# Up products of one block by Strassen's scheme, with VectorE work moved to make room for them

## The chip, the cores and the metric

The kernel runs on one core of a Trainium2 chip. A core has TensorE (PE, with its weight loads shown apart as PEld), VectorE (DVE), ScalarE (ACT), GpSimd (POOL), SyncE (SP) and 16 DMA engines. The metric is the device time of one execution in microseconds, lower is better.

## The reference, cut to what matters

A layer norm feeds two branches, and their sum with the input is the output. One branch is a diagonal complex state-space model over 2048 tokens, the other a gated feed-forward layer:

```python
def _B_ref(x, w1, w3, w2):
    gate = jnp.einsum("bsd,df->bsf", x, w1)      # 2048 x 512 times 512 x 1792
    up = jnp.einsum("bsd,df->bsf", x, w3)
    h = _silu(gate) * up
    return jnp.einsum("bsf,fd->bsd", h, w2)
# ... _A_ref: Bu = xn B_bar; h_t = Lam_bar h_{t-1} + Bu_t; y = 2 Re(C h) + Dskip xn
xn = _layernorm(x, axis=-1)
return x + _A_ref(xn, ...) + _B_ref(xn, ...)
```

## The kernel before

The tokens are cut into four blocks (0 to 3) of 512. For a block, 14 gate tiles and 14 up tiles of 128 features are computed, each by four matmuls of 512 columns. The inputs of the recurrence (the `bu` stage) are eight more tiles of four such matmuls in each block. The outputs are computed for pairs of 128-token chunks; there are eight pairs (0 to 7), two for each block. This last stage already uses Strassen's scheme, with seven products in place of eight.

```python
def mms(ps, w, f, tsl):                       # in glu(b): one gate or up tile
    for dt in range(NDT):                     # NDT = 4
        nc.tensor.matmul(out=ps[:, tsl], lhsT=w[:, dt, f * P:(f + 1) * P], rhs=xnT[:, dt, tsl], ...)
...
g_ps = ...; mms(g_ps, w1_sb, f, slice(0, TBLK))
u_ps = ...; mms(u_ps, w3_sb, f, slice(0, TBLK))
evac(f, g_ps, u_ps)                           # ACT: Silu of the one, Copy of the other
```

The sums for the output stage are made by VectorE, S1 among them, and S1 is used by the second product of a pair:

```python
def row_sums(n, b, p):
    ...
    return [... for out, x, z, op in ((s1, a21, a22, ALU.add), (a21, a11, a21, ALU.subtract),
                                      (s2, s1, a11, ALU.subtract))]
```

The recurrence is rotated into real scans by products with tables. A rotation uses a work buffer `p` of two (`ssmw`), and its sum is mostly made by a DMA that accumulates into its destination, so as to spare VectorE:

```python
st["p"] = ssmw.tile(FULL, BF16, name="p")                              # pre_a: waits until p is free
nc.vector.tensor_tensor(out=st["p"][...], in0=st["g"], in1=tabe[...], op=ALU.mult)
...
gp.dma_start(out=st["g"], in_=st["p"], accum_op=ALU.add)               # pre_c, blocks 1 to 3
...
gp.dma_start(out=act_state(b, hf), in_=st["p16"], accum_op=ALU.add)    # post_c, all blocks
```

The order of VectorE's work is set by the program: a small list scheduler in it (`bg`) decides where the background work of the recurrence, the residual and the sums stands.

## Time and profile before

| | before |
|---|---|
| median of 3 runs | 203.59 us (203.54 to 204.22) |
| span of the profiled execution | 202.6 us (that execution took 204.41 us, 0.8 over the median) |
| PE busy | 97% |
| DVE busy, first to last stretch | nearly full until about 162 us, then half idle |

First the busy shares of the whole execution from the page, and the slice rows of PE and DVE (40 slices of about 5 us; 9 is 90% or more).

```profile
PE 197.4 (97%) x1304; PEld 122.5 (60%) x1317; DVE 172.5 (85%) x242; ACT 125.1 (62%) x251; POOL 44.2 (22%) x68
...
PE   8899999999999999999999999999999999999994
...
DVE  3699699999999999989949999999999935584833
```

PE has no slack, and from slice 6 to slice 32 DVE has little (slice 21 holds the wait shown below). To see the stages, here are busy times in windows of the same execution. The columns are: window, its length, then busy time and number of instructions of PE, PEld, DVE, ACT and POOL (instructions that reach over an edge are counted, too), granted clock, DMA share, GB/s. The five windows are pairs 0 and 1; gate/up and recurrence inputs of block 2, with recurrence inputs of block 3; pairs 2 and 3; gate/up of block 3; pairs 4 and 5.

```profile
69.99:86.80 16.81, 16.81 (x156) 15.04 (x154) 16.45 (x24) 12.00 (x31) 5.67 (x6) 1.00 0.55 110
86.80:124.78 37.98, 37.77 (x174) 17.24 (x177) 35.01 (x37) 28.98 (x52) 7.86 (x8) 1.00 0.51 91
124.78:141.59 16.81, 16.81 (x155) 15.06 (x154) 16.71 (x24) 2.38 (x6) 2.58 (x3) 1.00 0.55 111
141.59:165.77 24.18, 24.02 (x112) 10.96 (x112) 21.84 (x26) 16.39 (x28) 3.45 (x4) 1.00 0.46 93
165.77:182.58 16.81, 16.81 (x155) 15.06 (x154) 10.69 (x18) 2.66 (x7) 0.00 (x0) 1.00 0.09 25
```

DVE is busy for 16.71 of 16.81 us right before the stage that the change rewrites, for 21.84 of 24.18 us in it, and for only 10.69 of 16.81 us after it. Two pairs take 16.81 us of matmuls when PE never waits; this number serves as the ruler below.

The chain that ended last, in order of time (start, length, what), runs through PE alone in block 3:

```profile
141.81 10.74 PE gu_ps L525 x49
152.55 0.05 issue
152.60 10.95 PE gu_ps L525 x50
163.56 0.05 issue
163.61 2.32 PE gu_ps L525 x10
```

DVE's waits show one for a work buffer that an accumulating DMA still reads (columns: who waited for whom, total us, times, longest):

```profile
DVE p L457 <- DMA act<-p: 2.6, 1, 2.6
```

### The profile page before, as it was taken

The page shows a single profiled execution, that of the slowest core. Times are in us where ns is not written, and L with a number is a line of the kernel's source. Part 1 is how long each engine was busy: PE and PEld are TensorE (multiplying, and loading weights), DVE is VectorE, ACT ScalarE, POOL GpSimd, SP SyncE. Part 2 cuts the span into 40 slices and gives each one's busy share as a digit, 9 for nine tenths or more (in the row PEclk, how much of TensorE's full clock was granted, in tenths as well). Part 3 has the DMA queues.
Part 4 walks back from the last instruction along what each step waited for, and adds up shares of the span by engine and source line. Part 5 has one row for each costly group of instructions (what it writes and reads, how often), then busy time and mean ns, then how long its engine had stood idle before and what let it go on. Part 6 is the DMA issues. An engine that isn't in the chain of part 4 may idle for free.

```text
span 202.6 us, 3438 instructions
## 1 busy us (share of the span) xinstructions
PE 197.4 (97%) x1304; PEld 122.5 (60%) x1317; DVE 172.5 (85%) x242; ACT 125.1 (62%) x251; POOL 44.2 (22%) x68
## 2 busy tenths in 40 slices
PE   8899999999999999999999999999999999999994
PEld 2774444444444588854444446888444458888993
DVE  3699699999999999989949999999999935584833
ACT  4699797699999966788866676110576662101010
POOL 7070279700310043352111010310101110000000
PEclk9999999999999999999999999999999999999999
DMA  6999996990573043926796004566330780101011
GB/s 165 320 258 217 290 172 143 319 273 2 101 146 66 0 78 74 170 98 106 93 188 125 11 19 88 99 135 133 91 65 0 153 160 1 52 3 52 29 40 39
DMA packets 28816, 23.16 MB, mean 114 GB/s; under 512 B 16128, under 2 KB 26496, under 8 KB 28800
## 3 DMA queue, kind: packets, MB, share of 16 engines
q1 hardware_dynamic: 25536, 13.21, 26.7%
q0 software_dynamic: 2688, 9.44, 24.9%
q10 hardware_dynamic: 576, 0.30, 0.5%
q8 instruction: 10, 0.16, 0.3%
q14 instruction: 6, 0.05, 0.1%
HBM read 7.74 MB, written 2.10 MB: 49 GB/s over the span
## 4 chain that ended last, share of the span: by engine, by line
PE 94%; DMA 2%; SPq 1%; DVE 1%; issue 1%
PE gu_ps L525 45%; PE gu_ps L724 16%; PE y_ps L724 9%; PE bu_ps L724 7%; PE y_ps L435 7%; PE bu_ps L435 7%; DMA w_sb<-in_B_w_dram 2%; PE gu_ps L557 2%; PE bu_ps L557 1%; DVE xn L735 1%; SPq L161 0%; PE y_ps L238 0%; SPq L151 0%; DVE x_blk L735 0%; SPq L163 0%
## 5 line engine op out<-in xcount | busy, mean ns | idle before, releaser
L525 PE MATMUL gu_ps<-xnT,w_sb 128*128 128x512 bf16 x415 | 91.9, 379 | 0.5
L525 PEld LDWEIGHTS <-w_sb 128*128 128x128 bf16 x424 | 41.4, 98 | 49.4
L724 PEld LDWEIGHTS <-act 128*128 128x128 f16 x451 | 43.2, 98 | 5.5
L534 ACT ACTIVATE g<-gu_ps 128x512 bf16<-128x512 f32 x55 | 33.1, 601 | 13.2 <-PE gu_ps L525 12.6
L535 ACT ACTIVATE u<-gu_ps 128x512 bf16<-128x512 f32 x55 | 33.2, 603 | 9.8 <-PE gu_ps L525 9.5
L435 PEld LDWEIGHTS <-bt 128*128 128x128 bf16 x128 | 12.5, 98 | 15.1
L543 DVE TENSOR_TENSOR act<-g,u 128x1024 f16<-128x1024 bf16 x28 | 19.0, 678 | 3.1 <-ACT u L535 3.1
L478 DVE TENSOR_TENSOR_SCAN u<-rho,act,u 128x512 bf16<-128x512 f32 x16 | 19.6, 1269 | 0.0
L492 POOL DMA_DIRECT2D act<-p x8 | 7.1, 887 | 42.3 <-DVE act L488 30.9
L435 PE MATMUL y_ps<-xnT,bt 128*128 128x512 bf16 x63 | 15.1, 379 | 0.1
L435 PE MATMUL bu_ps<-xnT,bt 128*128 128x512 bf16 x61 | 14.8, 379 | 0.1
L457 DVE TENSOR_TENSOR p<-u,tabe 128x2048 bf16<-128x2048 bf16 x8 | 9.8, 1221 | 2.7 <-DMA act<-p 2.6
L468 POOL DMA_DIRECT2D u<-p x6 | 5.3, 876 | 27.5 <-ACT u L535 7.9
L724 PE MATMUL y_ps<-tw,act 128*128 128x256 f16 x88 | 10.9, 273 | 0.0
L724 PE MATMUL gu_ps<-w_sb,act 128*128 128x256 bf16 (+1 forms) x84 | 10.8, 268 | 0.0
L724 PE MATMUL gu_ps<-tw,act 128*128 128x256 f16 x88 | 10.7, 273 | 0.0
L437 ACT ACTIVATE u<-bu_ps 128x512 bf16<-128x512 f32 x16 | 9.4, 597 | 2.0 <-PE bu_ps L435 1.6
L437 ACT ACTIVATE u<-y_ps 128x512 bf16<-128x512 f32 x16 | 9.5, 597 | 1.8 <-PE y_ps L435 1.3
L744 ACT ACTIVATE bu_ps<-y_ps 128x256 f32<-128x256 f32 x4 | 1.5, 369 | 13.7 <-PE y_ps L724 13.7
L461 DVE TENSOR_TENSOR u<-u,tabe 128x2048 bf16<-128x2048 bf16 x8 | 9.8, 1222 | 0.2
L478 DVE TENSOR_TENSOR_SCAN u<-rho,ends,u 128x512 bf16<-128x512 f32 x8 | 9.9, 1269 | 0.0
L484 DVE TENSOR_TENSOR p<-u,tabe 128x2048 f16<-128x2048 bf16 x8 | 9.8, 1221 | 0.1
(146 smaller groups left out, 279.6 us busy)
## 6 DMA issues: line engine op xcount, KB each, us to landing
act<-p POOLq DMA_DIRECT2D x8, 512.0 KB, 4.8
u<-p POOLq DMA_DIRECT2D x6, 512.0 KB, 4.9
xn<-x_blk POOLq DMA_DIRECT2D x4, 512.0 KB, 5.6
out_dram<-xn SPq DMA_DIRECT2D x15, 128.0 KB, 1.7
w_sb<-in_B_w_dram SPq DMA_DIRECT2D x1, 1792.0 KB, 7.9
w_sb<-in_B_w_dram SPq DMA_DIRECT2D x2, 768.0 KB, 6.3
w_sb<-in_B_w_dram SPq DMA_DIRECT2D x4, 256.0 KB, 4.9
w_sb<-in_B_w_dram SPq DMA_DIRECT2D x2, 512.0 KB, 6.2
```

Of the source, the lines that this page charges most:

```text
L435: nc.tensor.matmul(out=ps, lhsT=bt[:, ri, dt, pt * P:(pt + 1) * P], rhs=xnT_blk[b][:, dt, :], start=(dt == 0), stop=(dt == NDT - 1))
L437: nc.scalar.activation(out=u[:, j, ri, :], in_=ps, func=ACT.Copy)
L457: nc.vector.tensor_tensor(out=st["p"][:, :, ::-1, :], in0=st["g"], in1=tabe[:, psl, 2:0:-1, :], op=ALU.mult)
L461: nc.vector.tensor_tensor(out=st["g"], in0=st["g"], in1=tabe[:, psl, 0:1, :].to_broadcast(FULL), op=ALU.mult)
L478: nc.vector.tensor_tensor_scan(out=v, data0=rho[:, pt:pt + 1].to_broadcast([P, TBLK]), data1=v, initial=init, op0=ALU.mult, op1=ALU.add)
L484: nc.vector.tensor_tensor(out=st["p16"][:, :, ::-1, :], in0=st["g"], in1=tabe[:, psl, 1:3, :], op=ALU.mult)
L492: gp.dma_start(out=act_state(b, hf), in_=st["p16"], accum_op=ALU.add)
L525: nc.tensor.matmul(out=ps[:, tsl], lhsT=w[:, dt, f * P:(f + 1) * P], rhs=xnT[:, dt, tsl], start=(dt == 0), stop=(dt == NDT - 1))
L534: nc.scalar.activation(out=g16[:, f % 2, :], in_=g_ps, func=ACT.Silu)
L535: nc.scalar.activation(out=u16[:, f % 2, :], in_=u_ps, func=ACT.Copy)
L543: nc.vector.tensor_tensor(out=act(b)[:, k0:k1 + 1:k1 - k0, :], in0=g16, in1=u16, op=ALU.mult)
L724: nc.tensor.matmul(out=out, lhsT=left[:, k, :], rhs=right[k][:, cols], start=(start and k == 0), stop=(k == NK - 1), skip_group_check=True)
```

## The change

The intent is to save PE time in block 3. Twelve of its 14 up tiles form three groups of four tiles: 512 features by 512 inputs by 512 tokens, each halved. Strassen's scheme computes the group with seven products of half size in place of eight. A product is 2 x 2 matmuls of 256 columns. The sums of weights (S) and of tokens (T) are new VectorE work, and so are the sums of products that are read from PSUM, the memory that matmuls write. Accumulation in PSUM and copies by ScalarE do the rest of the recombination.

```diff
+    def up_sums(b):                          # on DVE: T1..T4 (128x512), S1..S3 (128x1536, all three groups)
+        ...
+    def glu_last(b):
+        def product(out, left, right, start):
+            for h in range(2):
+                for k in range(2):
+                    nc.tensor.matmul(out=out[:, h * TH:(h + 1) * TH], lhsT=left[:, k, h * P:(h + 1) * P],
+                                     rhs=right[:, k, :], ...)          # TH = 256 columns
+        ...                                   # tiles 12 and 13 as before
+        for n in range(NG):                   # NG = 3 groups; between the products stand the four gate tiles
+            product(g, a11, b11, True);  copy(f, g)
+            product(e, s1n, t1, True);   copy(s5, e)
+            gate_side(f0, upper[0])
+            product(f, a12, b21, False)
+            product(g, s2n, t2, False);  copy(e, g)
+            nc.vector.tensor_tensor(out=s4n, in0=a12, in1=s2n, op=ALU.subtract)
+            copy(upper[1][:, :, 0:TH], halves(f))
+            gate_side(f0 + 1, upper[0])
+            product(g, s3n, t3, False);  copy(z, g);  add(lower[1][:, :, TH:TBLK], g)
+            product(e, s4n, b22, False); add(upper[1][:, :, TH:TBLK], e)
+            gate_side(f0 + 2, lower[0])
+            product(z, a22, t4, False);  copy(lower[1][:, :, 0:TH], halves(z))
+            gate_side(f0 + 3, lower[0])
```

The rest makes room on VectorE and in time. S1 of pairs 2 to 5 is added in place by an accumulating DMA; S3 and S2 are formed without it; the products of pairs 2 to 7 stand in another order, so that S1 is used in the fifth product in place of the second (S2 stays in the fourth, which is now the first to need one of these sums). Three rotation buffers lie in blocks of `x` that are free by then. Two rotation sums go back to VectorE, and background work is put at other places:

```diff
+        return [(0.9, subtract(s3, a11, a21), ("sums", n)),
+                (0.9, lambda: ...vector add a21 += a22...) if n in (0, 1, 6, 7) else
+                (0.0, lambda: gp.dma_start(out=a21, in_=a22, accum_op=ALU.add), ("sums", n)),
+                (0.9, subtract(s2, a22, s3), ("sums", n))]
...
+        for i in ((1, 5, 2, 6, 4, 3, 7) if b == 0 else (1, 4, 2, 6, 5, 7, 3)):
+            products[i - 1]()                 # before: 1, 5, 2, 6, 4, 3, 7
...
-                st["p"] = ssmw.tile(FULL, BF16, name="p")
+                if b == NBLK - 1 or (b, hf) == (2, 1):
+                    st["p"] = x_blk[2 if b == 2 else 2 + hf].rearrange("p (j r) t -> p j r t", r=2)
+                else:
+                    st["p"] = ssmw.tile(FULL, BF16, name="p")
...
-                if b == 0:                    # pre_c on VectorE
+                if b == 0 or (b, hf) == (2, 0):
...                                           # post_c of (3, 1) on VectorE, too
+            if b == 0:
+                held.append((cl, o))          # stores of block 0 are issued after pair 1
```

More of the change, by code (lines that the diff above doesn't have):

```diff
@@ L95 @@
     MID = 8
+    NG = 3
+    TH = TBLK // 2
     LEAD = 2.0
@@ L125 @@
     bt = const.tile([P, 2, NDT, PS], BF16, name="bt")
+    bt_flat = bt.rearrange("p r t d -> p (r t d)")
     ct = const.tile([P, NPT, 2, D], FP16, name="ct")
@@ L441, in bu, with ssm_tasks @@
             bg.fill()
-    def ssm_tasks(b, posts_last=False, between=()):
+    def ssm_tasks(b, posts_last=False, between=(), middle=(), late=()):
         FULL = [P, 2, 2, TBLK]
@@ L491, in post_c @@
             def post_c():
-                gp.dma_start(out=act_state(b, hf), in_=st["p16"], accum_op=ALU.add)
+                if (b, hf) == (NBLK - 1, 1):
+                    nc.vector.tensor_tensor(out=act_state(b, hf), in0=act_state(b, hf), in1=st["p16"], op=ALU.add)
+                else:
+                    gp.dma_start(out=act_state(b, hf), in_=st["p16"], accum_op=ALU.add)
             pre_a.ready = lambda: (b, hf) in u_blk
@@ L498, in ssm_tasks @@
         (pre0, scans0, post0), (pre1, scans1, post1) = (half(hf) for hf in range(NPT // 2))
-        transfers = (post0[2], post1[2]) + ((pre0[2], pre1[2]) if b > 0 else ())
+        transfers = (post0[2],) + (() if b == NBLK - 1 else (post1[2],)) + ((pre1[2],) if b > 0 else ()) + ((pre0[2],) if b in (1, 3) else ())
         def add(*fns):
@@ L508, in ssm_tasks @@
             return
-        add(*pre0, *pre1)
+        add(*pre0)
+        for t in middle:
+            bg.add(*t)
+        add(*pre1)
         for t in between:
@@ L512, in ssm_tasks @@
         add(*scans0)
+        for t in late:
+            bg.add(*t)
         if posts_last:
@@ L606, in glu @@
             evac(f, g_ps, u_ps)
-            if b in (1, NBLK - 1) and f == NFT - 3:
-                seeds(0 if b == 1 else 4)
+            if b == 1 and f == NFT - 3:
+                seeds(0)
+            if b == 2 and f == 1:
+                bg.first(res_list(2))
             if b == 0 and f == FIRST:
@@ L613, in glu @@
             bg.tensor(1.72)
-            bg.fill()
+            bg.fill((4.0 if f < NFT - 3 else 1.0) if b == 2 else None)
             if pend and f % 2 == 0:
@@ L617, in glu, with up_quarter @@
         return gate
-    def res_tasks(b):
+    def up_quarter(kh, r, half=False):
+        v = w3_sb[:, 2 * kh:2 * kh + 2, 0:4 * NG * P].rearrange("p k (g r f) -> p k g r f", g=NG, r=2)[:, :, :, r, :]
+        return v.bitcast(FP16) if half else v
+    ups = {}
+    def up_sums(b):
+        xnT = xnT_blk[b]
+        n = 4 * NG * P
+        at = 2 * TBLK
+        s1, s2 = (bt_flat[:, at + i * n:at + (i + 1) * n].bitcast(FP16).rearrange("p (k g f) -> p k g f", k=2, g=NG)
+                  for i in range(2))
+        a11, a21, a22 = up_quarter(0, 0), up_quarter(0, 1), up_quarter(1, 1)
+        s3 = up_quarter(0, 1, True)
+        t = xtp.tile([P, NDT, TBLK], BF16, name="xnT").bitcast(FP16).rearrange("p a (k t) -> p a k t", k=2)
+        t1, t2, t3, t4 = (t[:, i] for i in range(4))
+        b11, b12, b21, b22 = (xnT[:, 2 * i:2 * i + 2, j * TH:(j + 1) * TH] for i in range(2) for j in range(2))
+        ups.update(s=(s1, s2, s3, up_quarter(1, 0, True)), t=(t1, t2, t3, t4), b=(b11, b12, b21, b22),
+                   s5=bt_flat[:, 0:2 * TBLK].bitcast(FP32))
+        return [(cost, lambda out=out, x=x, z=z, op=op: nc.vector.tensor_tensor(out=out, in0=x, in1=z, op=op), "up")
+                for cost, out, x, z, op in ((0.45, t1, b12, b11, ALU.subtract), (0.95, s1, a21, a22, ALU.add),
+                                    (0.45, t2, b22, t1, ALU.subtract), (0.95, s3, a11, a21, ALU.subtract),
+                                    (0.45, t3, b22, b12, ALU.subtract), (0.95, s2, s1, a11, ALU.subtract),
+                                    (0.45, t4, b21, t2, ALU.subtract))]
@@ new lines, in glu_last, with side, pair_tiles, copy @@
+    def glu_last(b):
+        xnT = xnT_blk[b]
+        s1, s2, s3, s4 = ups["s"]
+        t1, t2, t3, t4 = ups["t"]
+        b11, b12, b21, b22 = ups["b"]
+        s5 = ups["s5"]
+        def side(w, f):
+            ps = ps_gu.tile([P, TBLK], FP32, name="gu_ps")
+            for dt in range(NDT):
+                nc.tensor.matmul(out=ps, lhsT=w[:, dt, f * P:(f + 1) * P], rhs=xnT[:, dt, :],
+                                 start=(dt == 0), stop=(dt == NDT - 1))
+            bg.tensor(0.86)
+            return ps
+        def pair_tiles():
+            return glup.tile([P, 2, TBLK], BF16, name="g16"), glup.tile([P, 2, TBLK], BF16, name="u16")
+        def copy(out, x):
+            nc.scalar.activation(out=out, in_=x, func=ACT.Copy)
+        def gate_side(f, g16):
+            nc.scalar.activation(out=g16[:, f % 2, :], in_=side(w1_sb, f), func=ACT.Silu)
+        def gate(f, tiles):
+            bg.own(0.6, -0.5)
+            k0, k1 = k_gate(f), k_gate(f + 1)
+            nc.vector.tensor_tensor(out=act(b)[:, k0:k1 + 1:k1 - k0, :], in0=tiles[0], in1=tiles[1], op=ALU.mult)
+        def product(out, left, right, start):
+            for h in range(2):
+                for k in range(2):
+                    nc.tensor.matmul(out=out[:, h * TH:(h + 1) * TH], lhsT=left[:, k, h * P:(h + 1) * P],
+                                     rhs=right[:, k, :], start=(start and h == 0 and k == 0), stop=(k == 1),
+                                     skip_group_check=True)
+            bg.tensor(0.436)
+        def halves(ps):
+            return ps.rearrange("p (h t) -> p h t", h=2)
+        def add(out, ps):
+            bg.own(0.7)
+            nc.vector.tensor_tensor(out=out, in0=halves(ps), in1=halves(s5), op=ALU.add)
+        first = pair_tiles()
+        for f in range(4 * NG, NFT):
+            gate_side(f, first[0])
+            copy(first[1][:, f % 2, :], side(w3_sb, f))
+            bg.fill()
+        gates = [lambda: gate(NFT - 2, first)]
+        for n in range(NG):
+            f0 = 4 * n
+            a11, a12, a22, s1n, s2n, s3n, s4n = (v[:, :, n, :] for v in (
+                up_quarter(0, 0), up_quarter(1, 0), up_quarter(1, 1), s1, s2, s3, s4))
+            g, e = (ps_y.tile([P, TBLK], FP32, name="y_ps") for _ in range(2))
+            f, z = (ps_bu.tile([P, TBLK], FP32, name="bu_ps") for _ in range(2))
+            upper, lower = pair_tiles(), pair_tiles()
+            product(g, a11, b11, True)
+            copy(f, g)
+            product(e, s1n, t1, True)
+            copy(s5, e)
+            gate_side(f0, upper[0])
+            bg.fill(1.2)
+            gates.pop()()
+            product(f, a12, b21, False)
+            product(g, s2n, t2, False)
+            copy(e, g)
+            bg.own(0.42)
+            nc.vector.tensor_tensor(out=s4n, in0=a12, in1=s2n, op=ALU.subtract)
+            copy(upper[1][:, :, 0:TH], halves(f))
+            gate_side(f0 + 1, upper[0])
+            bg.fill()
+            product(g, s3n, t3, False)
+            copy(z, g)
+            add(lower[1][:, :, TH:TBLK], g)
+            product(e, s4n, b22, False)
+            add(upper[1][:, :, TH:TBLK], e)
+            gate_side(f0 + 2, lower[0])
+            bg.fill()
+            gate(f0, upper)
+            product(z, a22, t4, False)
+            copy(lower[1][:, :, 0:TH], halves(z))
+            gate_side(f0 + 3, lower[0])
+            bg.fill()
+            gates.append(lambda f0=f0, lower=lower: gate(f0 + 2, lower))
+        seeds(4)
+        return gates.pop()
@@ L621, in mul, with res_list @@
+    def res_list(b):
         def mul():
@@ L626, in add, with res_tasks @@
             gp.dma_start(out=xn_blk[b], in_=x_blk[b], accum_op=ALU.add)
-        bg.add(1.2, mul)
-        bg.add(0.0, add, ("res", b))
+        return [(1.2, mul, None), (0.0, add, ("res", b))]
+    def res_tasks(b):
+        for t in res_list(b):
+            bg.add(*t)
     def res_difference(b):
@@ L670, in sum_homes @@
         xs = [x_blk[i].rearrange("p c d -> p (c d)") for i in range(2)]
-        q = [v[:, n:n + 2 * DH].bitcast(FP32) for v in (*xs, bt.rearrange("p r t d -> p (r t d)"))]
+        q = [v[:, n:n + 2 * DH].bitcast(FP32) for v in xs]
+        q.append(const.tile([P, DH], FP32, name="q2"))
         return [[v[:, 0:n] for v in xs], [spare[:, 0:n], spare[:, n:2 * n]]], q
@@ L680, in row_sums, with subtract @@
         a21, a22 = a[:, 0:NK, r2], a[:, NK:2 * NK, r2]
-        s1, s2 = (v.bitcast(FP16).rearrange("p (k t) -> p k t", t=P) for v in homes[n % 2])
-        sums[n] = dict(a11=a11, a12=a12, a22=a22, s1=s1, s2=s2, s3=a21)
-        return [(0.9, lambda out=out, x=x, z=z, op=op: nc.vector.tensor_tensor(out=out, in0=x, in1=z, op=op), ("sums", n))
-                for out, x, z, op in ((s1, a21, a22, ALU.add), (a21, a11, a21, ALU.subtract),
-                                      (s2, s1, a11, ALU.subtract))]
+        s3, s2 = (v.bitcast(FP16).rearrange("p (k t) -> p k t", t=P) for v in homes[n % 2])
+        sums[n] = dict(a11=a11, a12=a12, a22=a22, s1=a21, s2=s2, s3=s3)
+        def subtract(out, x, z):
+            return lambda: nc.vector.tensor_tensor(out=out, in0=x, in1=z, op=ALU.subtract)
+        return [(0.9, subtract(s3, a11, a21), ("sums", n)),
+                (0.9, lambda: nc.vector.tensor_tensor(out=a21, in0=a21, in1=a22, op=ALU.add), ("sums", n)) if n in (0, 1, 6, 7) else
+                (0.0, lambda: gp.dma_start(out=a21, in_=a22, accum_op=ALU.add), ("sums", n)),
+                (0.9, subtract(s2, a22, s3), ("sums", n))]
     seeded = {}
+    held = []
     def seeds(n):
@@ L691, in seeds @@
         bg.flush(("res", b))
-        if n in (0, 3, 4, 6):
+        if n in (0, 3, 5, 7):
             f, e = (ps_bu.tile([P, TBLK], FP32, name="bu_ps") for _ in range(2))
@@ L699, in seeds @@
         if n == len(pairs) - 1:
-            spare = ps_bu.tile([P, TBLK], FP32, name="bu_ps")
+            spare = ps_gu.tile([P, TBLK], FP32, name="gu_ps")
             halves = [(t[:, 0:DH // 2], slice(i * DH // 2, (i + 1) * DH // 2)) for i, t in enumerate((e, spare))]
@@ L737, in store @@
         def store(cl, o, dsl=slice(0, D), eng=nc.sync):
-            eng.dma_start(out=ov[:, b * CPB + cl, dsl], in_=o[:, dsl])
+            if b == 0:
+                held.append((cl, o))
+            else:
+                eng.dma_start(out=ov[:, b * CPB + cl, dsl], in_=o[:, dsl])
         def right(cols):
@@ L744, in copy, with product1, product2 @@
             nc.scalar.activation(out=out, in_=x, func=ACT.Copy)
+        def product1():
+            mms(g, v["a11"], weight(0, D1), True)
+            copy(f, g)
+            if b > 0:
+                bg.first(list(then))
+            steps()
+            bg.fill()
+        def product2():
+            if b == 0:
+                bg.first(list(then))
+            mms(f, v["a12"], weight(1, D1), False)
+            v["s4"] = v["a12"]
+            bg.own(0.85, -1.1)
+            nc.vector.tensor_tensor(out=v["s4"], in0=v["a12"], in1=v["s2"], op=ALU.subtract)
+            add(o1[:, D1], f, o1[:, D1])
+            if last:
+                store(c1, o1, D1)
+            if n + 1 < len(pairs) and n not in (1, 3):
+                seeds(n + 1)
+            steps()
@@ new lines, in product3, with product4 @@
+        def product3():
+            for t, cols in halves:
+                mms(t, v["s4"], weight(1, D2), False, cols)
+                add(o1[:, right(cols)], t, q[0][:, cols])
+                if last:
+                    store(c1, o1, right(cols), nc.scalar if cols.stop == DH else nc.sync)
+            if not last:
+                store(c1, o1)
+            if b > 0:
+                steps()
+            bg.fill(0.5 if n == 1 else None)
+        def product4():
+            mms(z, v["a22"], tsum[3], True)
+            steps()
+            bg.fill(1.2 if b > 0 else None)
@@ L746, in product7, with product5, product6 @@
+        def product5():
+            for t, cols in halves:
+                mms(t, v["s1"], tsum[0], False, cols)
+                copy(q[1][:, cols], t)
+                steps()
+            if b > 0:
+                bg.fill(0.5 if n == 3 else None)
+        def product6():
+            mms(g, v["s2"], tsum[1], False)
+            add(q[0], g, o1[:, D2].bitcast(FP16))
+            steps()
+            bg.fill()
         def product7():
             mms(g, v["s3"], tsum[2], False)
-            add(q[0], g, o2[:, D1])
+            add(q[2], g, o2[:, D1])
@@ L749, in product7 @@
             add(o2[:, D2], g, q[1])
-            add(o2[:, D1], z, q[0])
+            add(o2[:, D1], z, q[2])
             store(c1 + 1, o2)
-        q_12 = q[2] if last else q[0]
-        mms(g, v["a11"], weight(0, D1), True)
-        copy(f, g)
-        steps()
-        bg.fill()
-        for t, cols in halves:
-            mms(t, v["s1"], tsum[0], False, cols)
-            copy(q[1][:, cols], t)
-            steps()
-        bg.first(list(then))
-        mms(f, v["a12"], weight(1, D1), False)
@@ L764, in y_fast @@
-        v["s4"] = v["a12"]
-        bg.own(0.85, -1.1)
-        nc.vector.tensor_tensor(out=v["s4"], in0=v["a12"], in1=v["s2"], op=ALU.subtract)
-        add(o1[:, D1], f, o1[:, D1])
-        if n + 1 < len(pairs) and n not in (1, 3):
-            seeds(n + 1)
-        steps()
-        mms(g, v["s2"], tsum[1], False)
-        steps()
-        add(q_12, g, o1[:, D2].bitcast(FP16))
-        bg.fill()
-        mms(z, v["a22"], tsum[3], True)
-        steps()
-        bg.fill()
-        if last:
-            store(c1, o1, D1)
-            product7()
@@ L781, in y_fast @@
-        for t, cols in halves:
-            mms(t, v["s4"], weight(1, D2), False, cols)
-            add(o1[:, right(cols)], t, q_12[:, cols])
-            if last:
-                store(c1, o1, right(cols), nc.scalar if cols.stop == DH else nc.sync)
-        steps()
-        if not last:
-            store(c1, o1)
-            bg.fill(0.5 if n in (1, 3) else None)
-            product7()
-            steps()
-            bg.fill()
+            if b == 0:
+                steps()
+                bg.fill()
@@ L794 @@
+        products = (product1, product2, product3, product4, product5, product6, product7)
+        for i in ((1, 5, 2, 6, 4, 3, 7) if b == 0 else (1, 4, 2, 6, 5, 7, 3)):
+            products[i - 1]()
     ln_alloc(0)
@@ L841 @@
     bg.first([(0.0 if kept else 0.2, keep_ends, ("ends", 0))])
+    bg.flush(("ends", 0))
     y_fast(0, row_sums(1, *pairs[1]))
@@ L845 @@
     sin_step(("ln", 2, True))
+    for cl, o in held:
+        nc.sync.dma_start(out=ov[:, cl, :], in_=o)
     res_difference(1)
-    ssm_tasks(2, between=row_sums(2, *pairs[2]))
+    ssm_tasks(2, between=row_sums(2, *pairs[2]), late=res_list(3))
     gate = glu(2)
@@ L850 @@
     sin_step(("ln", 3, True))
+    res_difference(2)
     seeds(2)
     bu(3)
-    res_tasks(2)
-    posts = ssm_tasks(3, True)
+    posts = ssm_tasks(3, True, between=up_sums(3))
+    res_difference(3)
+    posts()
     y_fast(2, row_sums(3, *pairs[3]))
@@ L857 @@
     y_fast(3, row_sums(4, *pairs[4]))
-    res_tasks(3)
-    res_difference(2)
-    posts()
-    res_difference(3)
-    gate = glu(3)
+    bg.flush("up")
+    gate = glu_last(3)
     gate()
     for n in range(4, len(pairs)):
+        ahead = row_sums(n + 1, *pairs[n + 1]) if n + 1 < len(pairs) else ()
         if n == 5:
-            bg.flush(("ssm", 3))
-            bg.flush(("res", 3))
-        y_fast(n, row_sums(n + 1, *pairs[n + 1]) if n + 1 < len(pairs) else ())
+            for t in ahead:
+                bg.add(*t)
+        y_fast(n, ahead if n != 5 else ())
 _INS = ['A_x', 'A_Lambda_re', 'A_Lambda_im', 'A_B_re', 'A_B_im', 'A_C_re', 'A_C_im', 'A_log_dt', 'A_Dskip', 'B_x', 'B_w1', 'B_w3', 'B_w2']
```

## The prediction

> **What bounds the kernel now.** TensorE. The chain that ended last gives PE 94% of the 202.6 us span. After the first inputs (7.4 us) matmuls run practically without a gap to 199.6 us, so time is the sum of matmul slots. In that chain, 49 gate/up matmuls of 512 columns take 10.74 us (0.219 each), 11 of 256 columns 1.20 us (0.109 each). The Trainium skill, "TensorE: Matmul & The Clock Gate" (Part 1), agrees: a warm matmul starts every N / 2.4 GHz plus about 2.5 ns, 215.7 ns at N = 512.
>
> **What the change removes from PE.** Twelve up tiles are 48 matmuls of 512 columns: 10.5 us. Strassen, 7 products for 8: 3 x 7 x 4 = 84 matmuls of 256 columns: 9.2 us. Gain 1.3 us, all on the critical path. Everything else only has to keep PE from waiting.
>
> **What it adds and moves.** DVE (windows view: 16.8 of 17 us busy in 125-142, 21.5 of 24 in 142-166, 10.9 of 17 in 166-183): T sums 4 x 0.42 us, S1 to S3 3 x about 0.95 (interpolated between 128x1408 at 0.89 and 128x1792 at 1.09), S4 3 x 0.42, six PSUM adds of 512 fp32 at about 0.69 (extrapolated from 0.29 at 128, 0.42 at 256), two rotation adds of 1.24 brought back from DMA: +12.4 us. Four S1 of 0.885 go to accumulating DMA: -3.5. Net +9 us. One DVE wait of 2.57 us for an accumulating DMA (at 102 us) goes: rotation buffers now lie in x blocks. DVE's idle time from 163 to 182 us is about 8 us, so the work just fits before the sums of pair 6; the new product order (S2 first used in the fourth product) gives those some 3.6 us more.
>
> ACT: a group has 10 evacuations of 0.60 us in 6.5 us of PE. The tightest link is the copy of G into E: it starts about 0.2 us after its product and must end before the next product on G, one 0.87 us gate tile later. It fits by under 0.1 us: I expect PE gaps of 0 to 0.15 us per group.
>
> DMA: S1 moves 128x1408 in 256-byte pieces. 512 KB transfers land after 4.8 us now; S1 is used over 6 us later, so it is hidden.
>
> **Predicted time.** 203.6 - 1.3 + about 0.2 of new gaps = 202.5 us; eight in ten between 201.9 and 203.9. Chances: faster by over 2% 0.01, within 2% 0.95, slower by over 2% 0.04.
>
> **What would show it.** 48 fewer 512-column matmuls and 84 more of 256 columns at the 0.109 us pitch; block 3's gate/up stage 1.2 us shorter, other stages equal. PE idle in that stage under 0.5 us. DVE busy about 9 us up, its idle in the last 40 us about 8 us less; PE not waiting for DVE at the start of the last two pairs. ACT busy about 3.5 us up. Four accumulating DMAs of about 350 KB landing within 6 us.
>
> **What would make it wrong.** DVE late: if its backlog is not worked off, PE waits at the first S1 product of group 0 (some 4 us into the stage) or at pair 6; each could cost 1 to 4 us. Or the copies to E, Z and S5 queue behind Silu on ACT, and each group stalls by 0.3 us or more. Or the S1 transfers land late behind other accumulating DMAs.

## The result, and the profile after

| | before | after |
|---|---|---|
| median | 203.64 us (203.54 to 204.22, 4 runs) | 202.97 us (202.71 to 203.19, 4 runs) |
| ratio | | 0.9961, 95% interval 0.9938 to 0.9983 |
| span of the profiled execution | 202.6 us | 201.1 us |

A ratio here and below is the mean time of one kernel's fast runs over that of the other kernel's fast runs of the same rounds, so it is not quite the ratio of the medians. By the medians the change is 0.67 us (0.3%) faster. The interval excludes 1. The measured time lies in the predicted range, 0.47 us over the predicted 202.5 us. All outputs are right.

The page of the changed kernel, the same lines:

```profile
PE 197.2 (98%) x1353; PEld 126.4 (63%) x1353; DVE 180.4 (90%) x256; ACT 127.2 (63%) x257; POOL 47.9 (24%) x70
...
PE   8999999999999999999999999999999999999994
...
DVE  4699699999999999989999989998989998988833
```

The windows of the changed kernel for the same five stages:

```profile
69.32:86.47 17.15, 16.97 (x155) 14.98 (x154) 16.56 (x25) 13.29 (x34) 4.66 (x7) 1.00 0.58 109
86.47:124.47 38.00, 38.00 (x177) 17.22 (x178) 37.26 (x39) 28.09 (x48) 9.29 (x9) 1.00 0.68 112
124.47:141.28 16.81, 16.81 (x156) 15.07 (x154) 15.44 (x24) 2.40 (x6) 5.71 (x4) 1.00 0.66 83
141.28:164.33 23.05, 23.05 (x151) 14.47 (x148) 22.09 (x32) 17.86 (x33) 0.86 (x1) 1.00 0.40 66
164.33:181.14 16.81, 16.81 (x155) 15.07 (x154) 15.09 (x24) 2.97 (x8) 2.84 (x2) 1.00 0.50 69
```

Put side by side by stage (us):

| stretch | before | after | difference |
|---|---|---|---|
| start to pair 0 | 69.99 | 69.32 | -0.67 |
| pairs 0 and 1 | 16.81 | 17.15 | +0.34 |
| block 2, inputs of block 3 | 37.98 | 38.00 | +0.02 |
| pairs 2 and 3 | 16.81 | 16.81 | 0 |
| gate/up of block 3 | 24.18 | 23.05 | -1.13 |
| pairs 4 to 7 and the end | 36.82 | 36.82 | 0 |

The first row is scatter between single executions: the profiled execution of the kernel before was 0.8 us over its median, and other traces of both codes have pair 0 start between 69.46 and 69.85 us. What remains, -1.13 + 0.34 + 0.02 = -0.77 us, fits the difference of the medians, -0.67 us. So two things are to be explained: the gain of 1.13 us in block 3, and a loss of 0.34 us before block 2, where the change seems to touch nothing.

In block 3 the chain in order of time now alternates between gate tiles (L671) and Strassen products (L693); the first group is:

```profile
141.44 3.45 PE gu_ps L671 x16
144.90 0.87 PE y_ps L693 x8
145.77 0.86 PE gu_ps L671 x4
146.63 0.44 PE bu_ps L693 x4
147.07 0.44 PE y_ps L693 x4
147.51 0.86 PE gu_ps L671 x4
148.37 0.89 PE y_ps L693 x8
```

A product takes 0.44 us, as planned. In the second and third group the product with S3 (the first half of a line like the last one) starts 0.03 us late, in the first 0.015 us; PE's records show no other gap over 0.01 us in the stage.

The loss is named by PE's waits (columns as above), and the chain has the same transfer in it for 5.46 us:

```profile
PEld L539 <- DMA xnT<-xn: 0.5, 1, 0.5
PE gu_ps L539 <- DMA xnT<-xn: 0.2, 1, 0.2
```

```profile
80.96 5.46 DMA xnT<-xn
86.42 0.05 issue
86.47 7.08 PE gu_ps L539 x32
```

The first gate matmuls of block 2 wait for the last of the four DMA transposes of the normalised block. In the kernel before this transfer landed just in time, by the trace's semaphore records 16.70 us after pair 0 started (17.11 us in the changed kernel): the first gate matmul starts 16.81 us after pair 0, which is the ruler exactly.

Of the DMA issues (KB each, median us from issue to landing), the accumulating ones of the recurrence and of S1, before and after (two `u<-p` at 5.1 us remain after; four `xn<-x_blk` of 512 KB for the residual, at 5.6 and 5.8 us, stand in both):

```profile
act<-p POOLq DMA_DIRECT2D x8, 512.0 KB, 4.8
u<-p POOLq DMA_DIRECT2D x6, 512.0 KB, 4.9
```

```profile
act<-p POOLq DMA_DIRECT2D x7, 512.0 KB, 5.2
u<-x_blk POOLq DMA_DIRECT2D x3, 512.0 KB, 6.5
act<-act POOLq DMA_DIRECT2D x4, 352.0 KB, 6.8
```

S1, the last line, moves fewer bytes in more time, 6.8 us for 352 KB: its pieces are 128 fp16, 256 bytes. The Trainium skill, "DMA: Bandwidth & Descriptors" (Specifications), asks for transfers of at least 512 B for line rate; this trace fits that, as a packet of 256 bytes of S1 lasts 55 ns and one of 4096 bytes of the others 340 ns, but no run tries another piece size. I had expected it to land within 6 us. It costs nothing, since PE does not wait for it.

### The profile page after: what moved, and what is told of

It reads as the page before. It is cut to its first block, busy times and chain, and to the rows that moved or that the text cites. A ratio compares the mean times of both kernels' runs of the same rounds, so it can differ in the third digit from the quotient of the medians.

```text
span 201.1 us, 3551 instructions
## 1 busy us (share of the span) xinstructions
PE 197.2 (98%) x1353; PEld 126.4 (63%) x1353; DVE 180.4 (90%) x256; ACT 127.2 (63%) x257; POOL 47.9 (24%) x70
## 4 chain that ended last, share of the span: by engine, by line
PE 59%; DVE 33%; DMA 3%; issue 2%; POOL 1%; ACT 1%; DVEq 0%
PE gu_ps L865 13%; PE gu_ps L539 12%; PE y_ps L865 7%; PE gu_ps L671 7%; PE bu_ps L865 4%; DVE u L484 4%; DVE act L557 4%; PE y_ps L438 3%; PE bu_ps L438 3%; PE y_ps L693 3%; DMA xnT<-xn 3%; DVE tw L796 2%; PE bu_ps L194 2%; DVE u L467 2%; DVE p L463 2%
## 5 line engine op out<-in xcount | busy, mean ns | idle before, releaser
L539 PE MATMUL gu_ps<-xnT,w_sb 128*128 128x512 bf16 x312 | 68.2, 379 | 0.2 <-DMA xnT<-xn 0.2
L539 PEld LDWEIGHTS <-w_sb 128*128 128x128 bf16 x312 | 30.4, 98 | 36.8 <-DMA xnT<-xn 0.5
L549 ACT ACTIVATE u<-gu_ps 128x512 bf16<-128x512 f32 x41 | 24.8, 606 | 5.8 <-PE gu_ps L539 5.1
L824 POOL DMA_DIRECT2D act<-act x4 | 8.0, 2002 | 33.8 <-DVE tw L820 28.9
L865 PE MATMUL gu_ps<-w_sb,act 128*128 128x256 bf16 (+3 forms) x126 | 15.9, 267 | 0.0
L671 PE MATMUL gu_ps<-xnT,w_sb 128*128 128x512 bf16 x64 | 15.9, 379 | 0.0
L557 DVE TENSOR_TENSOR act<-g,u 128x1024 f16<-128x1024 bf16 x21 | 14.2, 678 | 0.6 <-ACT u L549 0.6
L501 POOL DMA_DIRECT2D act<-p x7 | 6.3, 907 | 32.2 <-DVE act L494 28.2
L865 PE MATMUL bu_ps<-w_sb,act 128*128 128x256 bf16 (+3 forms) x84 | 10.4, 264 | 0.0
L865 PE MATMUL gu_ps<-ct,act 128*128 128x256 f16 (+1 forms) x72 | 10.4, 267 | 0.0
```

The lines of the kernel that those rows point to most:

```text
L549: nc.scalar.activation(out=u16[:, f % 2, :], in_=u_ps, func=ACT.Copy)
L557: nc.vector.tensor_tensor(out=act(b)[:, k0:k1 + 1:k1 - k0, :], in0=g16, in1=u16, op=ALU.mult)
L671: nc.tensor.matmul(out=ps, lhsT=w[:, dt, f * P:(f + 1) * P], rhs=xnT[:, dt, :], start=(dt == 0), stop=(dt == NDT - 1))
L865: nc.tensor.matmul(out=out, lhsT=left[:, k, :], rhs=right[k][:, cols], start=(start and k == 0), stop=(k == NK - 1), skip_group_check=True)
```

## The experiments

Twelve kernels ran in three calls, each call on one chip, with the kernel before timed beside them (median 204.17, 203.97 and 204.54 us in the three calls, 11 runs each). The kernel before differs by 0.6 us between calls, so times are compared by ratio to it, or within a call.

| kernel | median us | ratio to before | PE wait before block 2 (stretch of pairs 0 and 1 less 16.81), us |
|---|---|---|---|
| a1 no Strassen | 204.21 | 1.0001 (0.9984 to 1.0019) | 0.22 |
| a2 Strassen only | 206.17 | 1.0106 (1.0088 to 1.0124) | 0 |
| a3 two groups | 203.63 | 0.9979 (0.9961 to 0.9997) | 0.26 |
| a4 after, again | 203.46 | 0.9974 (0.9953 to 0.9995) | 0.42 |
| b1 stores later | 203.21 | 0.9977 (0.9945 to 1.0010) | 0.17 |
| b2 sum on VectorE, no transfer | 205.33 | 1.0065 (1.0053 to 1.0078) | 0 |
| b3 S1 on VectorE | 211.08 | 1.0339 (1.0309 to 1.0368) | 0.36 |
| b4 rotation in own buffers | 203.72 | 0.9980 (0.9962 to 0.9998) | 0.22 |
| c1 transfer after transposes | 202.96 | 0.9922 (0.9896 to 0.9949) | 0 |
| c2 after, third time | 203.22 | 0.9937 (0.9909 to 0.9965) | 0.04 |
| c3 old product order | 205.67 | 1.0059 (1.0029 to 1.0089) | 0.20 |
| c4 instruction fetch moved | 203.06 (one run) | | 0.08 |

### a1: everything but the Strassen products

```diff
-    posts = ssm_tasks(3, True, between=up_sums(3))
+    posts = ssm_tasks(3, True)
...
-    bg.flush("up")
-    gate = glu_last(3)
+    gate = glu(3)
+    seeds(4)
```

> The changed kernel with block 3's up products as plain matmuls again; everything else of the change stays. My theory: the Strassen products are all of the gain (84 slots of 256 columns at 0.109 us for 48 of 512 columns at 0.2155: 1.18 us, less 0.09 of gaps), and the rest of the change costs 0.3 us, because PE waits for the transposed block 2. So block 3's gate/up stage, from its first matmul to the first of pair 4, goes back from 23.05 to 24.13 us, and the time is about 204.05 us, 0.3 us slower than the kernel before. Rival: the other parts (product order, rotation buffers, S1 by DMA) give part of the gain by themselves; then the stage still returns to 24.1 us, but other stages are shorter and the time is at or under the kernel before (203.6 or less).

The ratio is 1.0001: the rest of the change has no gain of its own. Block 3's stage returned to 24.17 us, and every stage after block 2 kept its length. The stage in the chain of this run:

```profile
141.80 24.17 PE gu_ps L539 x112
```

The rival, that the other parts help by themselves, falls. My figure of 204.05 us assumed the kernel before at 203.6; it was at 204.17, and the loss that I expected against it (0.3 us) is within the interval but not shown by the time; the trace has a PE wait of 0.22 us. This trace also has all 112 records of the stage, so it gives the true slot: 24.17 / 112 = 0.2158 us, which is what the Trainium skill, "TensorE: Matmul & The Clock Gate" (Part 1), states to 0.1 ns or so (215.7).

### a2: the Strassen products alone, on the kernel before

```diff
+    ...up_quarter, up_sums, glu_last as in the change...
-    posts = ssm_tasks(3, True)
+    posts = ssm_tasks(3, True, between=up_sums(3))
-    gate = glu(3)
+    bg.flush("up")
+    gate = glu_last(3)
```

> The kernel before with only the Strassen products of block 3 added (their sums, the new stage), none of the relief for VectorE. My theory: VectorE was 16.8 of 17 us busy just before the stage and has to take some 10 us more, so it is late: PE waits at the first S1 product of group 0 or at the start of pair 4 or pair 6; 1 to 4 us lost against a gain of 1.1, time 203.5 to 206.5. Rival: VectorE's idle time after 163 us takes it all, and the time is 202.5 (1.1 us under the kernel before), better than the full change because block 2's transposes are not late.

It is 1.06% slower than the kernel before. PE's waits in this run after 120 us:

```profile
PE bu_ps L841 <- DVE x_blk L800: 1.6, 1, 1.6
PE gu_ps L841 <- DVE act L883: 0.9, 1, 0.9
PE y_ps L680 <- DVE bt L642: 0.3, 1, 0.3
```

The third line is the S1 product of group 0 (a gap of 0.49 us between PE's matmuls). The second is the product with S4 in pair 5, at 180 us (1.02 us), and the first is the S1 product of pair 6, at 185 us (1.81 us). Group 0 and pair 6 are the places that the prediction named for a VectorE that comes late; pair 5 is one more. The gain in PE slots is the same as in the full change, and 3.3 us are given back. So the Strassen products pay only together with the relief of VectorE. And, as expected, block 2's transposes were not late here.

### a3: two groups in place of three

```diff
-    NG = 3
+    NG = 2
...                                       # tiles 8 to 13 as plain tiles, in pairs
```

> The changed kernel with 8 gate tiles by Strassen in place of 12 (two groups). Theory that a group is worth its slots alone, 16 x 0.2155 - 28 x 0.109 = 0.39 us less 0.03 of gap: the stage takes 23.05 + 0.36 = 23.4 us, the time is 0.36 us over the changed kernel of the same call. Rival: the extra VectorE or ScalarE work of a group costs PE time elsewhere; then two groups are as fast as three or faster.

The stage took 23.43 us, against 23.05 us with three groups and 24.17 us with none: 0.37 to 0.38 us for each group. The median is 0.17 us over that of a4, less than the 0.38 us that the stage lost, but a4's profile had a longer wait before block 2 (0.42 against 0.26 us), and the intervals overlap. The stage lengths decide: a group is worth its slots, and nothing is given back elsewhere.

### a4 and c2: the changed kernel again

> The changed kernel unaltered, as the base for the other runs of this call. Expected 0.9961 of the kernel before, within 0.1%, and again a PE wait of 0.3 us (0.2 to 0.5) before the first gate matmul of block 2, if that wait is a property of the kernel; if it was chance in one execution, it is absent or under 0.1 us.

> The changed kernel unaltered, as the base of this call: 0.9961 to 0.9974 of the kernel before, PE wait before block 2 of 0.2 to 0.45 us.

There are three measurements: 0.9961, 0.9974 and 0.9937. The wait before block 2 was 0.34, 0.42 and 0.04 us: it varies from run to run of the same code. Over the ten profiles of kernels with the changed code and with the transfer beside the transposes (the first profile, a1, a3, a4, b1, b3, b4, c2, c3, c4) it is 0.23 us in the mean, from 0.04 to 0.42. In the two profiles of the old code for this stretch (before, a2) it is 0, and the last transpose landed 16.70 and 16.62 us after pair 0 started, against 16.80 to 17.19 us in the ten. Two profiles are few, but the two groups don't overlap.

### b1: the stores of block 0 issued later

```diff
-    for cl, o in held:
-        nc.sync.dma_start(out=ov[:, cl, :], in_=o)
...
             if b == 2 and f == 1:
                 bg.first(res_list(2))
+                for cl, o in held:
+                    nc.sync.dma_start(out=ov[:, cl, :], in_=o)
```

> The changed kernel, but the four stores of block 0 are issued after the second gate tile of block 2 and no longer right behind the transposes of block 2. Rival theory (contention with the stores delays the transposes): the PE wait before the first gate matmul of block 2 (0.2 to 0.4 us in the four runs of kernels with this code, none in the two of the old code) goes, and the time falls by 0.3 us against the changed kernel. My theory: the stores start only as the last transposes end, the delay comes from the 512 KB accumulating transfer ahead of them and a fetch of instructions; then the wait stays at 0.2 to 0.4 us.

The wait stayed, 0.17 us, and the ratio (0.9977) is that of a4 (0.9974), though one of the six runs took 205.14 us and widens its interval (0.9945 to 1.0010). The stores are not the cause. In the changed kernel, too, their packets start only as the last of the transposes' packets pass.

### b2: no accumulating transfer beside the transposes

```diff
-                if b == 0 or (b, hf) == (2, 0):
+                if b == 0 or (b, hf) in ((2, 0), (1, 1)):
                     nc.vector.tensor_tensor(out=st["g"], in0=st["g"], in1=st["p"], op=ALU.add)
...                                       # and the scheduler's list of transfers without this one
```

> The changed kernel, but the rotation sum of block 1, second half, is an add on VectorE (1.24 us) and no longer a 512 KB accumulating transfer that runs beside the transposes of block 2. My theory: the transposes land about 2 us earlier, well before pair 1 ends, so the PE wait before block 2 is 0 and the stretch from pair 0 to there is 16.81 us; time 0.3 us under the changed kernel, unless VectorE, 1.24 us later now, makes PE wait elsewhere (then a new gap in the following stages). Rival: the wait has nothing to do with that transfer; then it stays at 0.2 to 0.4 us.

Times from issue to landing of block 2's four transposes, in the first profile of the changed kernel and in this run:

```profile
DMA to landing us min/median/max: 2.4/4.0/6.4
```

```profile
DMA to landing us min/median/max: 2.4/2.5/3.1
```

The third now landed 12.9 us after the start of pair 0 (16.75 us in the changed kernel) and the last 14.8 us (17.11 us), and PE did not wait before block 2. So that transfer is what makes the transposes late. The counts of DMA packet records in each microsecond show it (packets of 256 bytes belong to the transposes, of 4096 to the accumulating transfer; c1 is described below):

```
us from start          78   79   80   81   82   83   84   85
changed: 256 B        512  349  236  439    0    0  369  143
changed: 4096 B         0    0    0   25   50   49    4    0
c1: 256 B             212  300  512  500  281  243    0    0
c1: 4096 B              0    0    0    0    0    0    0   32
```

In microseconds 82 and 83, while 99 of the 128 packets of 4096 bytes pass, no packet of the transposes moves, although 512 of their 2048 are still to come. The Trainium skill, "DMA: Bandwidth & Descriptors" (Queues, rings and completion order), says that a DMA engine goes round-robin between the queues it has work for, a whole packet at a time. (That the profile's packet records are the page's packets, which hold several descriptors each, is not shown.) In the trace of the kernel before that fits (about 24 packets of each kind in each half microsecond); in this one the smaller packets stood still. Whether they were held up behind the others or not yet handed to the engines can't be told from these records. Nor does this tell the old code from the changed one: in a4, the changed kernel again, the packets alternated and the wait was the longest, 0.42 us; in a2, with the old code, they stood still for 2.3 us and PE did not wait.

But b2 as a kernel was 2.1 us slower than b1, which is the changed kernel but for its stores. The reason teaches as much: VectorE had 1.24 us more to do at a time when it is full. PE's matmuls show new gaps of 0.93 us in pair 2, 0.39 and 0.65 us in group 0, and 0.74 us in pair 6. One add of 1.24 us cost more than its own length.

### b3: S1 of pairs 2 to 5 on VectorE

```diff
-                (0.9, lambda: ...vector add...) if n in (0, 1, 6, 7) else
+                (0.9, lambda: ...vector add...) if True else
```

> The changed kernel with S1 of pairs 2 to 5 as adds on VectorE (4 x 0.89 us) in place of accumulating transfers. My theory: the relief is needed, since VectorE has under 1 us of idle time from pair 2 to pair 5; PE waits 0.5 to 3 us, at group 0 of the Strassen stage or in pairs 4 to 6. Rival: the new product order alone gives enough slack, and the time is that of the changed kernel within 0.2 us.

It is 3.4% slower, far beyond what I expected. Part of that goes with a lower clock: three of the four runs had a granted clock of 0.991 to 0.992 and took 210.91 to 211.65 us, while the profiled one, at 1.0, took 209.76 us, 2.8% over the median of the kernel before. The four adds are 4 x 0.89 = 3.6 us; PE's waits in the profiled execution are:

```profile
PE gu_ps L865 <- DMA act<-p: 2.3, 1, 2.3
PE y_ps L693 <- DVE bt L655: 2.0, 2, 1.5
PE y_ps L865 <- DVE x_blk L876: 1.5, 1, 1.5
```

The last is in pair 3 (140.8 us), the second in group 0 (its first products with S1 and S2), and the first in pair 6 (188.7 us), which waits for the states of block 3: these come out of VectorE late and then still need an accumulating DMA. Between PE's matmuls the gaps at these places add up to 6.6 us, which is about what this run took over the median of b1 (203.21 us). The rival, that the new order gives enough slack, falls clearly.

### b4: rotation buffers back in the work buffers

```diff
-                if b == NBLK - 1 or (b, hf) == (2, 1):
-                    st["p"] = x_blk[...]...
-                else:
-                    st["p"] = ssmw.tile(FULL, BF16, name="p")
+                st["p"] = ssmw.tile(FULL, BF16, name="p")
```

> The changed kernel with the rotation buffers of (2,1), (3,0), (3,1) back in the two work buffers, in place of x blocks. My theory: VectorE waits for accumulating transfers to release these buffers again (one wait of about 2.6 us in the kernel before, around 102 us), and as VectorE is full until pair 6, 1 to 3 us of it reach PE at group 0 or in pairs 4 to 6. Rival: VectorE takes other work meanwhile and PE sees nothing: time within 0.2 us of the changed kernel.

VectorE's wait came back, and PE's followed:

```profile
DVE p L460 <- DMA act<-p: 2.1, 1, 2.1
```

```profile
PE gu_ps L862 <- DVE x_blk L873: 0.5, 1, 0.5
```

Between its neighbours' slots the gap in pair 2 is 0.65 us, and no other stage changed. The median is 0.5 us over that of b1, which differs from the changed kernel only in its stores; the two ratios (0.9980 and 0.9977) don't show a difference, so this rests on the trace. By the gap this part is worth about 0.65 us of PE time here; of the 2.1 us that VectorE waits, it makes up most without PE noticing, and my range of 1 to 3 us was too high.

### c3: the old order of products

```diff
-        for i in ((1, 5, 2, 6, 4, 3, 7) if b == 0 else (1, 4, 2, 6, 5, 7, 3)):
+        for i in ((1, 5, 2, 6, 4, 3, 7) if not last else (1, 5, 2, 6, 4, 7, 3)):
```

> The changed kernel with the product order of the kernel before in all pairs (S1 as second product, S2 as fourth). My theory: S1 of pairs 2 to 5 now comes from a transfer that lands 6.8 us after its issue, and pair 6 needs S1 from VectorE at once, so the order is part of what makes the change work: PE waits at the second product of pairs 2, 4, 5 or 6, 0.5 to 3 us in all. Rival: the sums are early enough in any order, and the time is that of the changed kernel within 0.2 us.

It is 0.6% slower than the kernel before. Weight loads that waited, in order of time (start, length, what, idle time before and what ended it):

```profile
134.82 2.30 PEld L865 LDWEIGHTS <-act 128*128 128x128 f16 x22 [0.77 <-DMA act<-act]
148.04 0.33 PEld L693 LDWEIGHTS <-bt 128*128 128x128 f16 x4 [0.49 <-DVE bt L655]
175.55 2.30 PEld L865 LDWEIGHTS <-act 128*128 128x128 f16 x22 [0.58 <-DMA act<-act]
188.64 1.41 PEld L865 LDWEIGHTS <-act 128*128 128x128 f16 x13 [1.06 <-issue]
```

The first and third are the second products of pairs 3 and 5, which wait for S1 from its transfer. The second is group 0, the fourth is the fifth product of pair 6, which waits for late work of VectorE (PE's own wait list has 0.9 us for an add there). As the edit also shifts the places of background work on VectorE, not all of it is the order alone; the two waits for S1's transfer are. S1 by DMA and the new order belong together.

### c4: an instruction fetch moved

```diff
+    pad = const.tile([P, 4], FP32, name="pad")
+    for _ in range(12):
+        nc.vector.memset(pad[:, 0:1], 0.0)
+        nc.gpsimd.memset(pad[:, 1:2], 0.0)
+    for _ in range(6):
+        nc.scalar.activation(out=pad[:, 2:3], in_=eps_t, func=ACT.Copy)
```

> The changed kernel with tiny idle instructions at the start of VectorE, GpSimd (12 each) and ScalarE (6), so that an 8 KB fetch of instructions that all kernels with the changed code have 15.3 to 15.7 us after pair 0 starts, and the two with the old code have not, falls earlier. Theory that this fetch is what delays the last transposes by 0.2 to 0.4 us: PE wait before block 2 is under 0.1 us if the fetch has moved by over 1 us. Rival: the delay comes from the accumulating transfer and other timing; then the wait stays at 0.2 to 0.4 us though the fetch has moved. The first microseconds of this kernel may be longer and don't count.

The fetch moved from 15.3 to 15.7 us after pair 0 to 14.0 us, and the wait was 0.08 us. But c2, the unaltered kernel, had only 0.04 us with the fetch at 15.3 us. One run inside the scatter tells nothing. Why the changed code has its last transpose land 0.3 us later on average than the old code (17.0 against 16.7 us after pair 0 started), with the same transfer beside them, stays open.

### c1: the transfer issued after the transposes

```diff
+                elif (b, hf) == (1, 1):       # pre_c: not now,
+                    deferred.append(lambda g=st["g"], p=st["p"]: gp.dma_start(out=g, in_=p, accum_op=ALU.add))
...
                 gp.tensor_scalar(out=nm, in0=sm, ...)         # statistics step of block 3 on GpSimd
+                if b == 3:                    # but here, in the same queue
+                    while deferred:
+                        deferred.pop()()
```

> The changed kernel, but the accumulating transfer of block 1, second half, is issued about 3.3 us later, behind the statistics step of block 3 on its queue, so it starts when the transposes of block 2 have landed. VectorE's program is unaltered. My theory: as in the run without this transfer, the transposes land 13 us after pair 0 starts, PE does not wait before block 2 (stretch of pairs 0 and 1 is 16.81 us), and because the transfer still lands before the scans that read it, nothing else moves: 0.3 us (0.2 to 0.45) under the changed kernel of the same call, about 0.9945 of the kernel before; this would be the version that beats both. Rival: the transfer then lands too late for the scans or shifts VectorE, and the 0.3 us come back as a wait in the next stages, as in the run with the add on VectorE.

VectorE's program has the same instructions in the same order as in the changed kernel; the transfer's issue moved from 10.3 to 14.1 us after the start of pair 0. The window of pairs 0 and 1 is back at the ruler, and the others are those of the changed kernel:

```profile
69.80:86.61 16.81, 16.81 (x155) 15.06 (x154) 16.41 (x24) 13.30 (x34) 4.46 (x6) 1.00 0.45 96
```

The last of the transposes landed 14.7 us after pair 0 started, 2.1 us before PE could use it, so this is slack and not luck. The median is 202.96 us against 203.22 us for c2, with runs from 202.65 to 203.24 against 202.67 to 203.78. The two ratios (0.9922 and 0.9937) have overlapping intervals, so the time does not prove the 0.26 us, and c2's own profile had a wait of only 0.04 us. What is shown is that the wait, 0.23 us in the mean of ten profiles, is gone in this trace with nothing given back in the later stages. By ratio it is the fastest version, clear of the kernel before but not of the changed kernel.

## Why the prediction was right or wrong

**The bound and the size of the gain: right.** PE bounded the kernel, and a saved slot was a saved 0.2158 us. The prediction took 1.3 us for the slots less 0.2 us for gaps; measured are 48 x 0.2158 - 84 x 0.109 = 1.20 us of slots less two gaps of 0.03 us, and the stage shrank by 1.13 us. The slot term was over-sized because 0.219 us came from a chain line with a missing record; the gap term was over-sized, too, and that the two errors cancelled was luck. a1 and a3 show that the gain is the Strassen products' alone, 0.37 us per group.

**VectorE: right, by a narrow margin.** Predicted were 9 us more work and 8 us less idle time in the last 40 us. Measured: busy time 172.5 to 180.4 us (+7.9), and idle time in the last 40 us from 18.6 to 9.9 us (8.7 less; 40 us less the busy time of a window over them). The work just fits, as said: PE does not wait for DVE in the stage or at the last pairs of the changed kernel, but with 3.6 us more (b3), 1.24 us more (b2) or 2.1 us of waiting (b4), PE waits at the places named under "what would make it wrong", group 0 and pair 6 (b2, b3), and in pairs 2 and 3 besides. Each such miss was said to cost 1 to 4 us; together they cost 6.6 us of PE time in b3's profiled run.

**"Other stages equal": this step failed.** Pairs 0 and 1 took 17.15 us for 16.81. The prediction checked the new transfers and sums and left the old transfers out, as if what was hidden before stayed hidden. The transposes of block 2 had at most 0.1 us of slack in the kernel before: the window view shows the stretch at exactly 16.81 us, but not that a transfer had landed at its very end. A landing some tenths later went straight to PE, 0.23 us on average. This, and not the Strassen stage, is why the first profile gained 0.77 us after the start where 1.1 us were predicted. b2 and c1 show that the transfer beside the transposes makes them late; what made the changed code later than the old one is open. That the time still fell near the forecast says little by itself: the range of 201.9 to 203.9 us held the 203.6 us of the kernel before, too. The stage lengths of a1 and a3 carry the proof.

**ScalarE: mechanism right, size off.** The copy of G into E was the tightest link; the product with S3, which waits for it, has the only gaps, 0.03 us in two of three groups where 0 to 0.15 were allowed. Busy time rose by 2.1 us and not by 3.5: a queued activation of 512 elements lasts 0.60 us in the trace but follows the one before after 0.5 us, and the sum of durations, which did rise by 3.5 us, counts the overlap twice.

**S1 by DMA: hidden, but slower than said.** It landed after 6.8 us and not within 6. The new order is what makes this harmless (c3).

## What to carry to other kernels

On an engine that never waits, count the slots from a stage whose records are complete, and the gain is known to a tenth of a microsecond; whether it arrives is decided by the second engine, so move work off it in the same change and look for the waits where its backlog would surface. Before calling other stages equal, look for transfers that now land just in time: their slack is next to nothing, and no busy share shows it. When small-packet transfers such as transposes share the DMA engines with a large transfer that is not yet needed, issue the large one after them; here (c1) that removed a wait of 0.04 to 0.42 us.

## What the Trainium skill lacked or had wrong

- "DMA: Bandwidth & Descriptors" (Queues, rings and completion order) states round-robin between queues by packets. In some traces 256-byte transpose packets did alternate with 4096-byte accumulating packets (24 of each in half a microsecond in the kernel before), in others, of the same code too, none moved for 2 us while about 100 of the large ones passed. The page has no number for a transpose beside such a transfer: the last two of four 128x512 transposes landed 2.4 and 3.1 us after their issue without it (b2, c1), and 4.0 to 6.4 us after with it.
- The same page (Specifications) has a smallest size for line rate, but no rate for accumulating transfers between places in SBUF. Here 512 KB landed after 4.8 to 6.5 us in the medians of the groups listed, and 352 KB in pieces of 256 bytes after 6.8 us.
